# Where two sets of weight sums stand in VectorE's order, in a four-layer attention and gated-unit kernel

## The chip, the core and the metric

The kernel runs on one core of one Trainium2 chip. A core has TensorE (PE) for matrix products, VectorE (DVE), ScalarE (ACT) and GpSimd (POOL) for elementwise work, and queues for DMA, of which SyncE's (SP) issues most transfers here. Each engine works through its own list of instructions in program order, and waits at an instruction until the semaphores it needs have been raised by other engines or by a DMA. The metric is the time of one execution on the device in microseconds (us), as the median of three runs.

## The reference

Four layers are applied to x (2048 rows of 1024): a linear attention and a gated feed-forward, then the same two again with the same weights. Each has a layer norm in front and a residual addition behind.

```python
def attention(x, wqkv, wo):            # 32 heads of 32
    q, k, v = split(x @ wqkv)
    phi = lambda t: where(t > 0, t + 1, exp(t)) + 1e-6
    kv, z = phi(k)^T v, sum over rows of phi(k)
    return (phi(q) kv / (phi(q) z + 1e-6)) @ wo

def gated(x, W_gate, W_up, W_down):    # 1024 -> 3584 -> 1024
    gate = relu(x @ W_gate)
    return (gate * (x @ W_up)) @ W_down

for layer in (attention, gated, attention, gated):
    x = x + layer(layernorm(x), ...)
```

## The kernel before: the parts that matter here

The gated layer computes its products with seven instead of eight block products per 2x2 block (a Winograd scheme), so that TensorE has an eighth less to do. For this each weight block needs sums and differences of its quarters (`make_gu`), and the input needs them too (`sums_x`). The first gated layer works through its first half of rows with sums that it makes itself on VectorE, and stores them to HBM (`tgu`); later passes load them ready-made.

```python
    def make_gu(self, t, w, u):          # sums of weight w ("g" or "u") of unit u
        v = self.nc.vector
        ...
        v.tensor_tensor(out=T[:, 0:2, :, :], in0=..., in1=..., op=ALU.subtract)   # L869, 128x1024
        v.tensor_tensor(out=T[:, 2, :, :], in0=..., in1=T[:, 0, :, :], op=ALU.subtract)  # L871, 128x512
        v.tensor_tensor(out=T[:, 3, :, :], in0=..., in1=T[:, 2, :, :], op=ALU.subtract)  # L872, 128x512
        self.later.at(3, lambda: self.nc.scalar.dma_start(out=self.tgu[w, u], in_=...))
```

`later.at(n, f)` calls f while the program is written, n steps further on (a step is one output tile, or one block product of four matmuls). Within a region the order of an engine's instructions is decided by a scheduler; `behind(it, f, args)` binds what f issues so that it stands after the instruction `it`.

```python
    def behind(self, it, fn, args):
        with self.tc.issue_after(it.ins):
            for a in args:
                fn(a)
```

The output projection of an attention layer makes 24 tiles of 128x512 in three quarters of eight (the last quarter is done differently, later). Each takes eight matmuls into one of four PSUM buffers (`ps`), and VectorE adds it onto the residual. The first quarter goes column half by column half over four row tiles, the others row tile by row tile.

```python
        def out_unit(sc, j, n2):
            t = sc * QT + j
            ps = self.ps.tile([P, NW], F32, tag="a")                 # 4 buffers
            for g in range(G):
                nc.tensor.matmul(ps, lhsT=pqT[sc][...], rhs=T[...], ...)          # L664
            ...
            if t < self.NS:                                          # quarters one and two
                self.last_x = nc.vector.scalar_tensor_tensor(out=xs, in0=ps, ..., in1=x0,
                                                  accum_out=...)                  # L675
            else:                                                    # quarter three
                self.last_x = nc.vector.tensor_tensor(out=xs, in0=x0, in1=ps, op=ALU.add)  # L679
```

Beside these VectorE reduces the attention's denominators (`z_sum`: L621, L622, L623, with GpSimd's products L616 and L628 on either side), finishes means of the layer norm (L205), whose rest is on ScalarE (L208 to L214), and makes the input sums s1 to s4 (`sums_x`: L908 to L911) from the transposed norms.

```python
            for sc in range(1, self.NQ - 1):
                if sc == 1:
                    for j in range(QT):
                        self.ln_at(2 * j + 2, last_ln, QT + j, 2)
                        later.at((11, 13, 15, 16)[j], lambda j=j: self.sums_x(last_ln, 0, j))
                ...
                if sc == 2 and l == 0:
                    for w, n in (("g", 2), ("u", 9)):
                        later.at(n, lambda w=w: self.make_gu(ring.get((last_ln, 0, w, 0)), w, 0))
                run(row_major(out_unit, sc))
```

The gated unit, fourteen block products. The first unit does them in the order one, two, five, six for gate and up in turn; then 7 and 3 for each, then 4 for each.

```python
        def five(w):                       # v = s1 * T0, kept as m5 (V)
            ...
            nc.scalar.activation(out=V[w], in_=v, func=ACT.Copy)
        def one(w):                        # x = first product, copied to y
            ...
            nc.scalar.activation(out=Y[w], in_=X[w], func=ACT.Copy)
        def two(w): ...
        def six(w):
            mm(w, 6, Y[w])
            Z[w] = self.ps.tile([P, NW], F32, tag="a", name=f"z{w}")
            nc.vector.tensor_tensor(out=Z[w], in0=Y[w], in1=V[w], op=ALU.add)     # L971
        ...
        for w in "gu":
            mm(w, 7, Y[w])
            nc.vector.tensor_tensor(out=V[w], in0=Y[w], in1=V[w], op=ALU.add)     # L984
            ...
            mm(w, 3, Z[w])
            ...
        for w in "gu":
            mm(w, 4, Y[w])
            ...
```

The layer around it asks for the weight sums of the next unit, where it has to make them itself:

```python
            for u in range(self.U):
                ...
                ring.load_to(ring.index((l, c, "g", u)) + 5)
                if first:
                    if u + 1 < self.U:
                        self.later.at(4 if u else 8, lambda u=u: behind(
                            self.last_put if u else self.last_x, lambda: [
                            self.make_gu(ring.get((l, c, w, u + 1)), w, u + 1) for w in "gu"]))
```

Of the kernel before, what the change touches and what calls it, by code (L numbers as in the profile page):

```python
# [8 lines left out]
ALU = mybir.AluOpType  # L9
# [80 lines left out]
class _Net:  # L90
# [337 lines left out]
    def layer_A(self, l, last_ln):  # L428
# [363 lines left out]
        with self.tc.manual_schedule(engines={mybir.EngineType.DVE, mybir.EngineType.Pool}):  # L792
            q3 = row_major(q_unit, self.NQ - 1)
            out0 = column_major(out_unit, 0)
            bring = self.bring_back if l else self.load_x
            ring.load_to(ring.index((l, "v1")) + 1)
            m_products(q3.pop(0))
            q3.insert(0, lambda: None)
            later.at(1, lambda: self.behind(ring.last, bring, range(self.NS)))
            for t in range(self.NS, self.ST - QT, 2):  # L800
                later.at(10 + t, lambda t=t: self.behind(self.last_turn, bring, (t, t + 1)))

            def with_fold(u, i):
                return lambda: (u(), fold_wo(i // 2) if i % 2 == 0 else None)

            run(q3[:2])
            run([with_fold(u, i) for i, u in enumerate(q3[2:] + out0[:1])])
            run(out0[1:3])
            ring.free_slowly((l, "o0"), later, 2)
            for i in range(11, self.ST):  # L810
                later.at(1 + 3 * (i - 11), lambda i=i: z_mult(*divmod(i, QT)))
            self.ln_later(last_ln, 0, 2, 2, 2)
            run(out0[3:])
# [5 lines that stand above are left out]
                if sc == 2 and l:  # L819
                    for j in range(QT):  # L820
                        later.at(11 + j, lambda j=j: q_turn(self.NQ - 1, j))
                    for t in range(self.ST - QT, self.ST):
                        later.at(3 + t, lambda t=t: self.behind(self.last_turn, bring, (t,)))
                if sc == 2 and l == 0:
                    for w, n in (("g", 2), ("u", 9)):
                        later.at(n, lambda w=w: self.make_gu(ring.get((last_ln, 0, w, 0)), w, 0))
                run(row_major(out_unit, sc))
            self.pairs = out_pairs(self.NQ - 1)
            self.turns = [] if l else [lambda j=j: q_turn(self.NQ - 1, j) for j in range(QT)] + [
                lambda t=t: self.behind(self.last_turn, bring, (t,)) for t in range(self.ST - QT, self.ST)]  # L830
# [88 lines left out]
    def glu(self, l, c, u, hT):  # L919

        nc, later = self.nc, self.later
        x1, x2 = self.xnT[l, 2 * c], self.xnT[l, 2 * c + 1]
        sa, sb = self.xs[l, c]
        A = {1: x1[:, 0:4, :], 2: x1[:, 4:8, :], 3: sb[:, 4:8, :], 4: x2[:, 4:8, :],
             5: sa[:, 0:4, :], 6: sa[:, 4:8, :], 7: sb[:, 0:4, :]}
        W = {}
        for w in "gu":
            t = self.ring.get((l, c, w, u))
            raw, T = self.raw_gu(t), self.sums_gu(t)
            W[w] = {1: raw[:, 0:4, 0:P], 2: raw[:, 4:8, 0:P], 3: raw[:, 4:8, P:2 * P],  # L930
                    4: T[:, 3, :, :], 5: T[:, 0, :, :], 6: T[:, 2, :, :], 7: T[:, 1, :, :]}

        def mm(w, m, ps, start=False):
            for k in range(4):
                nc.tensor.matmul(ps, lhsT=W[w][m][:, k, :], rhs=A[m][:, k, :],  # L935
                                 start=start and k == 0, stop=k == 3, skip_group_check=True)
            later.tick()

        h = hT[u // 2][:, (u % 2) * 4:(u % 2) * 4 + 4, :]
        V, X, Y, Z, R = {}, {}, {}, {}, {}  # L940

        def relu(out, ps):
            self.last_relu = nc.scalar.activation(out=out, in_=ps, func=ACT.Relu)  # L943

        def put(b, ps):
            self.last_put = nc.vector.tensor_tensor(out=h[:, b, :], in0=ps, in1=R.pop(b), op=ALU.mult)  # L946

        def five(w):
            v = self.kvp.tile([P, NW], F32, tag="kv0" if w == "g" else "kv1", name=f"v{w}")
            mm(w, 5, v, True)  # L950
            V[w] = self.temp(name=f"m5{w}")
            nc.scalar.activation(out=V[w], in_=v, func=ACT.Copy)  # L952

        def one(w):
            X[w] = self.ps.tile([P, NW], F32, tag="a", name=f"x{w}")
            mm(w, 1, X[w], True)
            Y[w] = self.ps3.tile([P, NW], F32, tag="b", name=f"y{w}")
            nc.scalar.activation(out=Y[w], in_=X[w], func=ACT.Copy)

        def two(w):  # L960
            mm(w, 2, X[w])
            if w == "g":
                R[0] = self.temp(name="r0")
                relu(R[0], X[w])
            else:
                put(0, X[w])

        def six(w):
            mm(w, 6, Y[w])
            Z[w] = self.ps.tile([P, NW], F32, tag="a", name=f"z{w}")  # L970
            nc.vector.tensor_tensor(out=Z[w], in0=Y[w], in1=V[w], op=ALU.add)  # L971

        if c == 0 and u == 0:
            for f in (one, two, five, six):
                for w in "gu":
                    f(w)
        else:
            for f, f2 in ((five, one), (two, six)):
                for w in "gu":
                    f(w)  # L980
                    f2(w)
# [3 lines that stand above are left out]
            if w == "g":  # L985
                relu(V[w], V[w])
            else:
                nc.gpsimd.tensor_tensor(out=h[:, 3, :], in0=V["u"], in1=V["g"], op=ALU.mult)  # L988
            mm(w, 3, Z[w])
            if w == "g":  # L990
                R[1] = self.temp(name="r1")
                relu(R[1], Z[w])
            else:
                put(1, Z[w])
        for w in "gu":
            mm(w, 4, Y[w])
            if w == "g":
                R[2] = self.temp(name="r2")
                relu(R[2], Y[w])
            else:  # L1000
                put(2, Y[w])
# [67 lines left out]
    def layer_B(self, l, final):  # L1069
        ring = self.ring  # L1070

        def behind(it, fn):
            with self.tc.issue_after(it.ins):
                fn()

        for c in range(2):
            hT = []
            first = l == 1 and c == 0
            wd = {}
            for u in range(self.U):  # L1080
                if u % 2 == 0:
                    hT.append(self.slot(f"h{l}_{c}_{u // 2}", dtype=F16))
                ring.load_to(ring.index((l, c, "g", u)) + 5)
                if first:
                    if u + 1 < self.U:
                        self.later.at(4 if u else 8, lambda u=u: behind(self.last_put if u else self.last_x, lambda: [
                            self.make_gu(ring.get((l, c, w, u + 1)), w, u + 1) for w in "gu"]))
                    if u in (3, 7):
                        d = self.U - 4 + u // 4 * 2
                        wd[d] = self.load_d(d)  # L1090
                    if 3 < u < 12:
                        self.later.at(4, lambda d=self.U - 4 + (u - 4) // 4 * 2, n=(u - 4) % 4: behind(
                            self.last_put, lambda: self.sums_d(wd[d], d, (n,))))
                if c == 0 and u == 1:
                    for n, turn in enumerate(self.turns):
                        self.later.at(1 + n, turn)
                if c == 0 and u in (1, 2):
                    self.later.at(6, lambda u=u: behind(self.last_put, self.pairs[u - 1]))
                self.glu(l, c, u, hT)
                if c == 0 and u == 2:  # L1100
                    self.pairs[2]()
                if c == 0 and u == (self.U - 1 if first else 0):
                    after = self.last_put.ins
            if c == 0:
                self.ln_chunk(l, 1, 20, 3, 3, after)
            elif not final:
                self.ln_later(l + 1, 0, 28, 6, 4)
            self.down(l, c, hT, final)
# [68 lines left out]
```

## Time and profile before

| | |
|---|---|
| time, median of 3 runs | 1475.59 us (1473.76 to 1477.6) |
| profiled span | 1474.3 us |
| TensorE busy | 1461.8 us, 99% |
| VectorE busy | 842.7 us, 57% |
| ScalarE busy | 578.2 us, 39% |
| GpSimd busy | 285.2 us, 19% |
| weight sums on VectorE (L869) | 28 sets, from 187.2 to 383.0 us |

The profile comes from one execution. Busy time of an engine is a share of the whole span; a matmul of 128x512 takes part in a pipeline, so that its listed duration (379 ns) is longer than the 216 ns after which the next one starts. A row of a table of waits says which engine stood still at which line, and what released it. A row of a table by stretch gives, for each engine, its busy time and its number of instructions in that stretch, then the clock that was granted to TensorE (1.00 is full), the mean busy share of the DMA engines and GB/s.

### The profile page before, as it was taken

To read this page: it belongs to the slowest core of one execution; us is meant where nothing else is said; L and a number is where in the kernel's file an instruction comes from. 1 tells how busy PE (TensorE), PEld (TensorE's weight loads), DVE (VectorE), ACT (ScalarE), POOL (GpSimd) and SP (SyncE) were. 2 spreads that over 40 slices of the span, in tenths; PEclk is the share of its full clock that TensorE was granted. 3 is DMA by queue.
4 is the path that set the end of the run, shared out by engine and by line. 5 is a ranking of instruction groups with operands and counts; after the bars stand their busy time and mean duration, and the time that the engine had idled before them with its cause. 6 is when DMAs were issued, how large, how long until landed. Compare 5 with 4: busy or idle time off the path is not lost.

```text
span 1474.3 us, 18704 instructions
## 1 busy us (share of the span) xinstructions
PE 1461.8 (99%) x6959; PEld 663.5 (45%) x6959; DVE 842.7 (57%) x1483; ACT 578.2 (39%) x1027; POOL 285.2 (19%) x190
## 2 busy tenths in 40 slices
PE   9999989999999999999999999999999999999999
PEld 4444434444444444444444444444444444444444
DVE  7978588666594433346368655766435433443632
ACT  6772564333330233341057726633333203333300
POOL 1354860011100011110023466410111001111000
PEclk9999999999999999999999999999999999999999
DMA  9940769654558954445943019976444687444461
GB/s 257 264 151 11 183 163 223 194 199 158 203 177 239 341 179 130 148 132 185 293 100 72 1 29 266 246 234 197 143 143 150 175 254 256 144 146 147 152 204 43
DMA packets 318363, 255.51 MB, mean 173 GB/s; under 512 B 105792, under 2 KB 291392, under 8 KB 317376
## 3 DMA queue, kind: packets, MB, share of 16 engines
q1 hardware_dynamic: 308304, 234.00, 54.6%
q10 hardware_dynamic: 9968, 20.32, 3.6%
q8 instruction: 54, 0.88, 0.3%
q14 instruction: 37, 0.30, 0.1%
HBM read 195.04 MB, written 34.60 MB: 156 GB/s over the span
## 4 chain that ended last, share of the span: by engine, by line
PE 94%; DVE 3%; DMA 1%; issue 1%; POOL 1%; ACT 0%; SPq 0%; DVEq 0%; POOLq 0%
PE ps L454 13%; PE dy L1034 10%; PE yg L935 10%; PE yu L935 10%; PE dx L1034 7%; PE dv L1034 7%; PE xu L935 6%; PE xg L935 6%; PE ps L664 4%; PE zu L935 3%; PE zg L935 3%; PE vu L935 3%; PE vg L935 3%; PE my L538 3%; PE mv L538 2%; PE mx L538 2%
## 5 line engine op out<-in xcount | busy, mean ns | idle before, releaser
L935 PEld LDWEIGHTS <-w 128*128 128x128 f16 (+1 forms) x3136 | 306.7, 98 | 372.2 <-issue 2.3
L988 POOL TENSOR_TENSOR h<-m5u,m5g 128x512 f16<-128x512 f32 x56 | 71.1, 1270 | 811.7 <-DVE m5u L984 756.4
L454 PE MATMUL ps<-w,xnT 128*128 128x512 bf16 x1024 | 223.6, 379 | 0.7 <-DMA w<-in_A_wqkv_dram 0.5
L1034 PEld LDWEIGHTS <-h 128*128 128x128 f16 x1120 | 109.6, 98 | 132.2
L454 PEld LDWEIGHTS <-xnT 128*128 128x128 bf16 x1024 | 99.4, 98 | 120.8 <-issue 1.5
L971 DVE TENSOR_TENSOR zg<-yg,m5g 128x512 f32<-128x512 f32 x56 | 39.1, 699 | 191.3 <-PE yg L935 191.3
L935 PE MATMUL yg<-s,w 128*128 128x512 f16 x448 | 115.0, 379 | 1.3 <-DVE zg L971 1.2
L935 PE MATMUL xg<-xnT,w 128*128 128x512 f16 x448 | 115.0, 379 | 0.0
L935 PE MATMUL xu<-xnT,w 128*128 128x512 f16 x448 | 115.0, 379 | 0.0
L935 PE MATMUL yu<-s,w 128*128 128x512 f16 x448 | 115.0, 379 | 0.0
L943 ACT ACTIVATE m5g<-m5g 128x512 f32<-128x512 f32 x56 | 35.2, 629 | 189.6 <-DVE m5g L984 189.6
L1034 PE MATMUL dy<-w,h 128*128 128x512 f16 x448 | 98.0, 379 | 0.0
L1034 PE MATMUL dx<-w,h 128*128 128x512 bf16 x448 | 97.3, 379 | 0.0
L401 ACT ACTIVATE e<-e,eps 128x512 f32<-128x512 f32 x128 | 92.4, 722 | 4.2
L400 ACT ACTIVATE e<-ps 128x512 f32<-128x512 f32 x128 | 75.8, 592 | 44.6 <-PE ps L454 43.7
L664 PE MATMUL ps<-T,pqT 128*128 128x512 bf16 x384 | 85.6, 384 | 4.9 <-DVE x L675 4.9
L616 POOL TENSOR_TENSOR kvc<-pq,kvc 128x1024 f32<-128x1024 bf16 x32 | 73.7, 2304 | 66.3 <-DVE den L621 42.3
L952 ACT ACTIVATE m5g<-vg 128x512 f32<-128x512 f32 x56 | 33.4, 597 | 111.7 <-PE vg L935 86.1
L473 POOL TENSOR_TENSOR kvc<-kvc,slab 128x512 f32<-128x512 f32 x46 | 58.0, 1268 | 75.6 <-DVE slab L404 59.6
L946 DVE TENSOR_TENSOR h<-yu,r 128x512 f16<-128x512 f32 x56 | 38.7, 691 | 56.8 <-PE yu L935 56.8
L984 DVE TENSOR_TENSOR m5u<-yu,m5u 128x512 f32<-128x512 f32 x56 | 38.7, 691 | 53.0 <-PE yu L935 53.0
L1034 PEld LDWEIGHTS <-e 128*128 128x128 f16 x448 | 43.9, 98 | 52.8
(154 smaller groups left out, 1966.8 us busy)
## 6 DMA issues: line engine op xcount, KB each, us to landing
w<-in_B_W_gate_dram SPq DMA_DIRECT2D x56, 512.0 KB, 5.8
w<-in_B_W_up_dram SPq DMA_DIRECT2D x56, 512.0 KB, 5.1
w<-td SPq DMA_DIRECT2D x32, 896.0 KB, 4.7
w<-in_B_W_down_dram SPq DMA_DIRECT2D x24, 896.0 KB, 5.2
w<-tg SPq DMA_DIRECT2D x42, 512.0 KB, 6.9
w<-tu SPq DMA_DIRECT2D x42, 512.0 KB, 5.4
w<-in_A_wqkv_dram SPq DMA_DIRECT2D x10, 1024.0 KB, 8.5
away<-x SPq DMA_DIRECT2D x16, 512.0 KB, 4.1
```

Source lines behind the costliest of these rows:

```text
L400: nc.scalar.activation(out=e, in_=ps, func=ACT.Relu, scale=-1.0)
L401: nc.scalar.activation(out=e, in_=e, func=ACT.Exp, scale=-1.0, bias=self.eps6[:, 0:1])
L454: nc.tensor.matmul(by_row(ps), lhsT=self.xnT[l, l_q][:, kt, j * P:(j + 1) * P], rhs=w[:, kt, :].rearrange("p (b i d) -> p i b d", i=R, d=H ...
L473: nc.gpsimd.tensor_tensor(out=ksum[:, cols], in0=ksum[:, cols], in1=pk, op=ALU.add)
L538: nc.tensor.matmul(banks[j], lhsT=A(i)[:, j * P:(j + 1) * P], rhs=B(i), start=start and i == 0, stop=i == NS - 1, skip_group_check=True)
L616: nc.gpsimd.tensor_tensor(out=prod, in0=pq_of[sc, j], in1=zrow, op=ALU.mult)
L664: nc.tensor.matmul(ps, lhsT=pqT[sc][:, g, j * P:(j + 1) * P], rhs=T[g // 4][:, g % 4, n2 * NW:(n2 + 1) * NW], start=(g == 0), stop=(g == G ...
L935: nc.tensor.matmul(ps, lhsT=W[w][m][:, k, :], rhs=A[m][:, k, :], start=start and k == 0, stop=k == 3, skip_group_check=True)
L946: self.last_put = nc.vector.tensor_tensor(out=h[:, b, :], in0=ps, in1=R.pop(b), op=ALU.mult)
L971: nc.vector.tensor_tensor(out=Z[w], in0=Y[w], in1=V[w], op=ALU.add)
L988: nc.gpsimd.tensor_tensor(out=h[:, 3, :], in0=V["u"], in1=V["g"], op=ALU.mult)
L1034: nc.tensor.matmul(banks[j], lhsT=A(k)[:, j * P:(j + 1) * P], rhs=w[:, i, :], start=start and k == 0, stop=k == self.U - 1, skip_group_che ...
```

## The change

Two sets of weight sums get other anchors. The sums of the first gated unit were asked for in the third quarter of the output projection, without an anchor, so that the scheduler was free to place them; now they are asked for in the second quarter, each behind the residual addition that is the latest at that moment. The sums of the second unit were bound to the last residual addition; now they are bound to the latest addition of partial products (L971 in the kernel before) in the first unit, and asked for one step later. For this `six` keeps its addition as `last_z`. The aim is that the sums stand in VectorE's order where their weights have come and nothing urgent is behind them.

```diff
@@ layer_A, around the output projection @@
-                if sc == 2 and l == 0:
-                    for w, n in (("g", 2), ("u", 9)):
-                        later.at(n, lambda w=w: self.make_gu(ring.get((last_ln, 0, w, 0)), w, 0))
+                if sc == 1 and l == 0:
+                    for w, n in (("g", 3), ("u", 10)):
+                        later.at(n, lambda w=w: self.behind(
+                            self.last_x, lambda w: self.make_gu(ring.get((last_ln, 0, w, 0)), w, 0), (w,)))
                 run(row_major(out_unit, sc))
@@ glu, six @@
-            nc.vector.tensor_tensor(out=Z[w], in0=Y[w], in1=V[w], op=ALU.add)
+            self.last_z = nc.vector.tensor_tensor(out=Z[w], in0=Y[w], in1=V[w], op=ALU.add)
@@ layer_B @@
-                        self.later.at(4 if u else 8, lambda u=u: behind(self.last_put if u else self.last_x, lambda: [
+                        self.later.at(4 if u else 9, lambda u=u: behind(self.last_put if u else self.last_z, lambda: [
                             self.make_gu(ring.get((l, c, w, u + 1)), w, u + 1) for w in "gu"]))
```

The lines of the kernel after are one further down from the first edit on (the output projection keeps L664, L675 and L679): L870, L872 and L873 are the weight sums there, L909 to L912 the input sums, L936 the block products, L972 and L985 the additions.

## The prediction

> **What bounds the kernel now.** I read the page first, then the waits of TensorE, then the chain that ended last around the longest wait, then the order of work on VectorE, then tables by stretch.
>
> Parts 1 and 2 of the page: the engine that sets the end, its share of the span, and the clock it was granted in 40 slices.
>
> ```profile
> PE 1461.8 (99%) x6959; PEld 663.5 (45%) x6959; DVE 842.7 (57%) x1483; ACT 578.2 (39%) x1027; POOL 285.2 (19%) x190
> PEclk9999999999999999999999999999999999999999
> ```
>
> TensorE (PE) is busy for 1461.8 of 1474.3 us, so a change off TensorE can save some 12 us at most, plus what TensorE does at less than full speed. The waits of TensorE, with total, number and longest in us:
>
> ```profile
> PE ps L664 <- DVE x L675: 4.9, 2, 2.7
> PE idle L272 <- DVE e L269: 1.3, 1, 1.3
> PE yg L935 <- DVE zg L971: 1.2, 1, 1.2
> ```
>
> Two of them lie where the change acts: 4.9 us in the output projection of the first attention layer (L664, waiting for a residual addition) and 1.2 us in the first gated unit (L935, waiting for zg). The chain that ended last (start, us, what), from 181 us on, says why the first exists:
>
> ```profile
> 181.38 5.83 DMA w<-in_B_W_up_dram
> 187.21 0.02 issue
> 187.23 0.04 DVE w L869
> 187.27 0.57 issue
> 187.84 0.69 DVE x L675 x2
> 188.53 1.13 DVE den L621
> 189.66 0.33 DVE w L871
> 190.00 2.01 DVE den L622
> 192.01 0.33 DVE w L872
> 192.34 0.26 DVE den L623
> 192.60 0.56 DVE x L675 x2
> 193.16 0.04 issue
> 193.21 1.01 PE ps L664 x3
> ```
>
> The first weight sum of the up weights (L869) stands in VectorE's order after three of the eight residual additions of the first quarter. Its operand is still on the way from HBM until 187.2 us. VectorE therefore does nothing from 181.0 to 187.2 us, though the fourth output tile is ready for its addition; the accumulators (four buffers) stay full and TensorE stops for 2.17 us before one tile and 2.73 us before the next. It also costs clock. Busy time by stretch, with the granted clock as last but two figures:
>
> ```profile
> 192.00:194.00 2.00, 0.79 (x3) 0.29 (x3) 1.97 (x9) 0.56 (x1) 1.32 (x1) 0.92 0.39 160
> 194.00:196.00 2.00, 2.00 (x6) 0.76 (x5) 1.93 (x6) 1.87 (x6) 1.38 (x2) 0.50 0.33 119
> 196.00:198.00 2.00, 2.00 (x8) 0.83 (x7) 2.00 (x9) 1.98 (x3) 2.00 (x2) 0.73 0.63 122
> ```
>
> TensorE did six and eight matmuls in stretches in which it does eleven elsewhere.
>
> The best yardstick is in the kernel itself: the second attention layer has the same output projection followed by the same gated unit, but takes its weight sums ready-made from HBM. The same table, from the second output tile to the first gated unit and over that unit, for layer two, layer one, layer one, layer two:
>
> ```profile
> 910.90:950.64 39.74, 39.74 (x197) 18.01 (x185) 31.41 (x76) 26.76 (x54) 21.91 (x11) 1.00 1.03 245
> 175.88:222.52 46.64, 41.73 (x198) 18.41 (x186) 35.87 (x83) 26.19 (x54) 29.80 (x15) 0.96 0.66 150
> 222.52:236.25 13.73, 12.42 (x57) 5.38 (x56) 11.11 (x24) 4.67 (x8) 1.27 (x1) 1.00 1.24 265
> 950.64:962.89 12.25, 12.25 (x58) 5.48 (x57) 7.24 (x14) 4.67 (x8) 1.27 (x1) 1.00 1.11 274
> ```
>
> **What the Trainium skill says.** "DVE: scalar operands, raw-bit mode, write accounting and state across instructions", section Flops that outlive an instruction, calls VectorE's queue one in-order queue; the 6.2 us of idleness in front of ready work agree. "TensorE: Matmul & The Clock Gate", section What's actually happening, says that an idle array falls to half its clock and needs about 3.4 us of work to return; the trace has 0.50 after the two waits, over some 3.2 us (194.0 to 197.0 us, a weight load every 0.43 us instead of 0.21). "SBUF — State Buffer", section Who interferes with whom, says that a VectorE operation with two SBUF inputs and a GpSimd operation exclude each other, and the later one waits for the whole of the other. Here L871, normally 0.42 us, took 2.01 us at 215.36 while GpSimd's L628 ran from 214.92 to 217.08. "VectorE: DVE Perf Modes", section The perf-mode tier table, gives tensor_tensor on 16-bit data in SBUF the double rate, 1224 ns for 2048 elements; the trace has 1.22 us for 2048, 0.68 for 1024 and 0.42 for 512, so one set of three sums is about 1.3 us of VectorE start to start.
>
> **The change part by part.** No instruction is added or removed: 28 sets of sums stay. Only places change, and the order of the changed kernel as built shows them.
>
> (a) Sums of the first gated unit. The up set leaves its place between the third and fourth addition of quarter one. The gate set now follows the first addition of the sixth tile row (tile x6, second quarter), the up set follows both additions of the ninth (x9, third quarter). Both weights were requested at about 181 us and landed at 187; the new places are reached after 193 us and after 205 us, so no wait for HBM remains. What goes is: 2.17 + 2.73 = 4.90 us of waits, the half clock (15 matmuls at 0.43 instead of 0.216 us = 3.2 us, half lost: 1.6), and 0.4 us of restarts and small gaps. The yardstick gives the sum: 46.64 - 39.74 = 6.90 us, if the stretch runs as in layer two. Does it? VectorE there has 31.41 us of work in 39.74 and takes on two sets, 2.6 us; that fits in the total. The gate set falls where VectorE in layer two waits for TensorE by 0.9, 0.15, 0.7 and 1.0 us per addition (930 to 940 us), so with one GpSimd operation of 1.9 us in its way (L628 runs just there, 929.06 to 930.98) it makes additions about 2 us late. Four accumulator buffers of 1.73 us each cover that. The up set falls at the point that corresponds to 941 us, and from there VectorE has no idle time until the input sums are done at 953.7. It pushes these by 1.3 us. The last s1 sum of the inputs starts at 952.20 in layer two, done at 952.62; TensorE wants it for vg at 954.10. Slack 1.5 us, less 1.3 for the up set, less a possible remainder from the gate set and a lock. I charge 0.3 us.
>
> (b) Sums of the second gated unit (two interleaved sets, 237.13 to 239.67 in unit two of the kernel before: 2.54 us). Before, part of them sit between the last input sums and zg, which makes TensorE wait 1.25 us. Now all six follow zu. The unit would run as in layer two (12.25 instead of 13.73 us: 1.48 us), were it not that the six sums now stand in front of the read of yg by m5g (L984). In layer two zu starts at 957.82, so VectorE is free at 958.42; plus 2.54 is 960.96; m5g takes yg until 961.65. TensorE wants to accumulate onto yg again at 961.16. That is 0.5 us of a new wait. The up weights of unit two must be there: their load follows the last normalised transposes, at 945.45 in layer two, 13 us ahead of need, with 5 to 8 us to land. I charge nothing.
>
> (c) Everything after, 1100 us of it, has TensorE at 99% or more and the same orders, so it moves forward by what was gained.
>
> Sum: 6.90 + 1.48 - 0.3 - 0.5 = 7.6 us. 1475.59 - 7.6 = 1468.0 us, 0.5% faster.
>
> **Rivals.**
>
> The lock moves the wait. If a GpSimd operation catches the up set or the gate set leaves VectorE late, the input sums end up to 2 us later and TensorE waits for vg. For it: VectorE is saturated just there, and L908 took 1.87 us at 943.37 beside L628 in layer two. Against it: L628 in front of the up set ends at 941.2, as the set begins. Time then 1469.5 to 1470.
>
> ScalarE becomes the bound. Its eight layer norms run without a break from 193.44 to 217.3 us, and the gated unit needs all eight. If they kept that time, TensorE would wait for them and gain little: about 1473. Against it: their first one waits 14.8 us for a mean that stands behind the stalled VectorE; in layer two they start 8.1 us after the second output tile, which is 184.0 us here, and end 33.2 us after it, at 209.1.
>
> The new place waits for a transfer. VectorE's order has the up sums of unit two directly after zu; if their load, or a store that holds its slot, is late by a few us, m5g and with it TensorE stand still. Time 1470 to 1473. Against: the 13 us above, and the load's issue moves forward along with ScalarE's norms.
>
> Nothing gained. The 4.9 us could have been slack for a later wait; but the other waits in TensorE's table (1.3, 0.6, 0.5 and 0.2 us) lie in the first 31 us, and none is listed after the first gated unit, so I give it little.
>
> **Range and chances.** The most to be had is 8.38 us (both stretches as in layer two), 1467.2; runs of the kernel before scatter over 3.8 us, so the median can lie 1.5 us off: low end 1465.5. The rivals' middle gives the high end, 1472. Two per cent is 29.5 us; neither way is such a change in sight: faster 0.005, within 0.99, slower 0.005.
>
> **What would show it.** Right: no wait of L664 on L675 in TensorE's table; clock 1.00 from 176 us to the gated unit; that unit starting near 215.6 us in place of 222.5; layer norms on ScalarE from about 184; no VectorE wait for the up weights; a wait of about 0.5 us of yg on m5g L985 in place of zg. Wrong: a wait of vg on an input sum of over 1 us, VectorE idle in front of a weight sum until a load lands, or L664 waiting for the additions around the gate set. The prediction fails as a whole if the gated unit starts after 219 us.

## The result, and the profile after

| | before | after |
|---|---|---|
| time, median (lowest to highest) | 1475.75 us (1473.76 to 1477.6) | 1468.79 us (1468.5 to 1468.92) |
| profiled span | 1474.3 us | 1466.7 us |
| TensorE busy | 1461.8 us | 1458.0 us |

The ratio of the times is 0.9953, with a 95% interval of 0.9936 to 0.997: some 7 us less, within 2%. The time was predicted as 1468.0 us (1465.5 to 1472.0).

The first rows of the page of the kernel after, engine totals and granted clock. TensorE (PE) is still busy for 99% of the span. The digits of the clock look as before, for a slice of 37 us is too coarse for a dip of 3 us; its loss shows only in short stretches.

```profile
PE 1458.0 (99%) x6920; PEld 663.1 (45%) x6959; DVE 844.1 (58%) x1483; ACT 578.4 (39%) x1027; POOL 285.8 (19%) x190
PEclk9999999999999999999999999999999999999999
```

TensorE's waits in the kernel after (total, number, longest, in us). The 4.9 us of L664 on L675 are gone, and so are the 1.2 us on zg. In their place stand 0.8 us of L664 on a residual addition of quarter three, and 0.3 us of vg on an input sum; the others of the table lie in the head of the kernel.

```profile
PE ps L664 <- DVE x L679: 0.8, 1, 0.8
...
PE vg L936 <- DVE s L909: 0.3, 1, 0.3
```

The table by stretch of the kernel after: from the second output tile to the first product of the first gated unit, over that unit to the first product of unit two, and two microseconds right behind the gate sums.

```profile
174.90:215.62 40.72, 39.67 (x194) 18.00 (x185) 37.29 (x82) 26.51 (x54) 29.33 (x15) 1.00 0.82 189
215.62:229.34 13.72, 13.47 (x62) 5.76 (x61) 11.44 (x25) 4.78 (x8) 1.27 (x1) 1.00 1.16 231
194.00:196.00 2.00, 2.00 (x11) 0.88 (x10) 1.93 (x3) 2.00 (x4) 0.95 (x1) 1.00 1.00 339
```

The first stretch took 40.72 us in place of 46.64 before and 39.74 in layer two, at full clock, with eleven matmuls in two microseconds where there were six. In layer two TensorE is busy for all of the 39.74 us, so the yardstick is its own work and nothing else. VectorE (DVE) is busy for 37.29 of the 40.72 us, more than in layer two plus two sets of sums (31.41 + 2.6 = 34.0). The prediction gave the unit as the stretch to the last products, one block short of unit two (13.73 and 12.25 us); for a comparison over the whole unit, to the first product of unit two, these are the rows of the kernel before, for layer one and layer two:

```profile
222.52:237.11 14.59, 13.28 (x61) 5.78 (x60) 11.70 (x25) 4.67 (x8) 1.27 (x1) 1.00 1.24 266
950.64:963.75 13.11, 13.11 (x62) 5.87 (x60) 7.84 (x15) 4.67 (x8) 1.27 (x1) 1.00 1.10 282
```

So unit one fell from 14.59 to 13.72 us and did not reach 13.11. From unit two to the end nothing moved: 1474.3 - 237.11 = 1237.2 us before, 1466.7 - 229.34 = 1237.4 after. The two stretches give 5.92 + 0.87 = 6.79 us; the rest of the difference of the profiled spans, 0.98 us, lies ahead of the second output tile (175.88 against 174.90), where the change touches nothing.

What became of VectorE's 34.0 us? One part was there before: layer one's stretch holds seven reductions of denominators (L621, with L622 and L623 behind each), layer two's only six, in both kernels. One such round takes 1.7 us of VectorE. The rest shows in the order of work on VectorE and on GpSimd (POOL), kernel after (start, duration, operation), with the gate set, the up set and the first input sum:

```profile
193.12 2.38 DVE L870 TENSOR_TENSOR w<-w 128x1024 f16<-128x1024 bf16 x1
...
205.28 1.85 DVE L870 TENSOR_TENSOR w<-w 128x1024 f16<-128x1024 bf16 x1
...
210.24 1.88 DVE L909 TENSOR_TENSOR s<-xnT 128x512 f16<-128x512 f16 x1
```

```profile
193.04 1.90 POOL L628 TENSOR_TENSOR pq<-pq,den 128x1024 bf16<-128x1024 bf16 x1
...
204.66 1.92 POOL L628 TENSOR_TENSOR pq<-pq,den 128x1024 bf16<-128x1024 bf16 x1
...
209.92 1.91 POOL L628 TENSOR_TENSOR pq<-pq,den 128x1024 bf16<-128x1024 bf16 x1 [3.34 <-DVE den L623]
```

Each of the three VectorE operations starts inside a product of GpSimd and ends 0.3 to 0.6 us after it. This waiting is called the lock below. Alone they last 0.68, 0.68 and 0.42 us (in the kernel before), so they lost 1.70, 1.17 and 1.46 us. The last of these is no new loss, for in layer two the same sum takes 1.87 us. The gate set was expected to be caught in this way, the up set was not. Together: 31.41 + 2.6 + 1.7 + 1.70 + 1.17 = 38.6 us of work, in a stretch of some 40. VectorE did 37.29 of it in the stretch; the gated unit began with two residual additions fewer done than in layer two (five of L679 against seven).

### The profile page after: what moved, and what is told of

It is laid out like the page before. It is cut to its first block, busy times and chain, and to the rows that moved or that the text cites. A ratio compares the mean times of both kernels' runs of the same rounds, so it can differ in the third digit from the quotient of the medians.

```text
span 1466.7 us, 18659 instructions
## 1 busy us (share of the span) xinstructions
PE 1458.0 (99%) x6920; PEld 663.1 (45%) x6959; DVE 844.1 (58%) x1483; ACT 578.4 (39%) x1027; POOL 285.8 (19%) x190
## 4 chain that ended last, share of the span: by engine, by line
PE 96%; DVE 2%; ACT 0%; issue 0%; DMA 0%; DVEq 0%
PE ps L454 15%; PE dy L1035 10%; PE yg L936 10%; PE yu L936 10%; PE dv L1035 7%; PE dx L1035 7%; PE xg L936 6%; PE xu L936 6%; PE ps L664 4%; PE zu L936 3%; PE zg L936 3%; PE vu L936 3%; PE vg L936 3%; PE my L538 3%; PE mv L538 2%; PE mx L538 2%
## 5 line engine op out<-in xcount | busy, mean ns | idle before, releaser
L936 PEld LDWEIGHTS <-w 128*128 128x128 f16 (+1 forms) x3136 | 306.7, 98 | 371.5 <-issue 1.6
L972 DVE TENSOR_TENSOR zg<-yg,m5g 128x512 f32<-128x512 f32 x56 | 39.2, 699 | 192.7 <-PE yg L936 192.7
L936 PE MATMUL yg<-s,w 128*128 128x512 f16 x448 | 115.0, 379 | 0.1
L936 PE MATMUL yu<-s,w 128*128 128x512 f16 x448 | 115.0, 379 | 0.0
L936 PE MATMUL xg<-xnT,w 128*128 128x512 f16 x448 | 115.0, 379 | 0.0
L936 PE MATMUL xu<-xnT,w 128*128 128x512 f16 x448 | 115.0, 379 | 0.0
L616 POOL TENSOR_TENSOR kvc<-pq,kvc 128x1024 f32<-128x1024 bf16 x32 | 73.6, 2299 | 61.7 <-DVE den L621 37.6
L664 PE MATMUL ps<-T,pqT 128*128 128x512 bf16 x374 | 83.2, 379 | 1.4 <-DVE x L679 0.8
L985 DVE TENSOR_TENSOR m5u<-yu,m5u 128x512 f32<-128x512 f32 x56 | 38.7, 691 | 52.0 <-PE yu L936 52.0
```

The source lines that it names most:

```text
L616: nc.gpsimd.tensor_tensor(out=prod, in0=pq_of[sc, j], in1=zrow, op=ALU.mult)
L664: nc.tensor.matmul(ps, lhsT=pqT[sc][:, g, j * P:(j + 1) * P], rhs=T[g // 4][:, g % 4, n2 * NW:(n2 + 1) * NW], start=(g == 0), stop=(g == G ...
L972: self.last_z = nc.vector.tensor_tensor(out=Z[w], in0=Y[w], in1=V[w], op=ALU.add)
```

## The experiments

Times are medians; "before" in a ratio is the kernel before, run beside. The stretches named are those of the two rows above: second output tile to gated unit, and the unit.

**Is it VectorE's idleness that costs, and how much can it lose for nothing?** The theory: TensorE stops because VectorE stands still ahead of the fourth residual addition, and any occupation of VectorE there does the same, beyond a slack. The rival lays the cost of the old place to the transfers themselves. Three kernels are the kernel after with 5, 10 or 15 statistics of 128x512 (`bn_stats`) put into VectorE's order ahead of the fourth addition. They need nothing from HBM; their output is not used.

```diff
+    if l == 0:                       # N = 5, 10, 15
+        with issue_after(self.last_x.ins):          # third addition
+            for _ in range(N):
+                self.fill = nc.vector.bn_stats(out=fill[:, 0, :], in_=self.x[0][:, 0:NW])
+    # the fourth addition is issued behind self.fill
```

> The kernel after, with five extra BatchNorm statistics (0.60 us each start to start, 3.0 us) put into VectorE's order between the third and fourth residual addition of quarter one, where the up sums stood before. Theory 1, VectorE's order: the fourth addition is then done near 184 us, its buffer is wanted by TensorE near 185.3 us, so no wait: 1468.5 to 1469.5 us. Theory 2, the gain has another source (transfers or stores spread differently, layer norms): also about 1468.8. It sets the zero of the series.

> The same with ten statistics, 6.0 us. Theory 1: the fourth addition ends near 186.7 us, TensorE waits 1.4 us for it and 0.5 us for the next, 1.9 us in two pieces; without a fall of the clock about 1470.7, with one about 1472.3 us. Theory 2: 1468.3 to 1469.5 us, since no transfer is moved.

> The same with fifteen, 9.0 us, about what the kernel before lost there (6.2 us idle, 0.6 us of work, 2.4 us of two more sums and of the lock). Theory 1: TensorE waits 4.3 us and 0.5 us, and the half clock of 1.6 us follows, less up to 1 us of the later waits of the kernel after, which vanish: 1473.8 to 1475.5 us. Theory 2: under 1470.5 us.

| statistics | held on VectorE | time (n) | ratio to before (95%) | stretch |
|---|---|---|---|---|
| none (the kernel after) | 0 | 1468.79 (4) | 0.9953 (0.9936 to 0.997) | 40.72 |
| 5 | 3.61 us | 1471.2 (9) | 0.9974 (0.9964 to 0.9984) | 42.78 |
| 10 | 7.25 us | 1474.43 (12) | 0.9997 (0.9989 to 1.0006) | 46.42 |
| 15 | 10.90 us | 1478.3 (14) | 1.0022 (1.0014 to 1.003) | 50.06 |

A statistic took 0.73 us, start to start, where 0.60 had been expected. TensorE's waits on residual additions in the kernel with five (L676 and L680 are L675 and L679 there) and the place of the one on L676, then the longest in the kernel with ten:

```profile
PE ps L664 <- DVE x L680: 1.8, 2, 1.6
...
PE ps L664 <- DVE x L676: 0.7, 1, 0.7
```

```profile
201.88 10.52 PE L664 MATMUL ps<-T,pqT 128*128 128x512 bf16 x48 [0.72 <-DVE x L676]
```

```profile
PE ps L664 <- DVE x L676: 2.4, 1, 2.4
```

Holding VectorE for 7.25 us, with no transfer in it, brings back the time of the kernel before, where it had stood idle for 6.2. That speaks against the transfers as the cause of the old loss. (Beside the idle time the kernel before had the up sums in that place, and L622 at 2.10 us; the kernel with ten has its sums and their lock later. The two are alike in size, not item by item.) But five were to cost nothing, and that was wrong: they cost 2.06 us of the stretch out of 3.61 (57%), and every five more cost 3.64 us, all that they took. So ten and fifteen also came out above their ranges. VectorE has some 1.5 us to give in this stretch of 40 us, not the depth of four accumulators. With five, VectorE was held from 180.1 to 183.7 us, and TensorE did not wait there at all: on the spot the four accumulators covered 3.6 us. It waited later, 0.72 us at 201 us behind the gate set, and 1.79 us at the additions of quarter three.

The kernels with ten and fifteen also show the clock. The table by stretch, kernel with ten, two stretches of two microseconds after its idle time of 2.45 us, which ended at 188.0 us:

```profile
188.00:190.00 2.00, 2.00 (x7) 0.82 (x7) 1.93 (x4) 0.00 (x0) 0.84 (x1) 0.68 0.00 0
190.00:192.00 2.00, 2.00 (x7) 0.60 (x6) 1.74 (x6) 1.45 (x3) 2.00 (x2) 0.50 0.00 0
```

Seven matmuls in two microseconds, at 0.68 and 0.50 of the clock. This fall added nothing to the time here: the step from five to ten, which brought it, cost 3.64 us, just what the statistics took, and TensorE still waited 1.8 us for VectorE at quarter three.

**One part alone.** The kernel before with only the second unit's sums moved, and the kernel after with only those moved back.

```diff
 # second unit alone: the kernel before, with
-   self.later.at(4 if u else 8, ... self.last_put if u else self.last_x ...
+   self.later.at(4 if u else 9, ... self.last_put if u else self.last_z ...
 # first unit alone: the kernel after, with
-   self.later.at(4 if u else 9, ... self.last_put if u else self.last_z ...
+   self.later.at(4 if u else 8, ... self.last_put if u else self.last_x ...
```

> The kernel before with only the second unit's sums moved behind the additions of partial products. Theory 1: the two waits for the residual additions and the half clock stay (waits of 4 to 5 us in TensorE's table), the wait of 1.2 us for zg goes, 0 to 0.5 us come back as a wait of yg on m5g: 0.7 to 1.2 us under the kernel before, about 1474.7. Rival: this part alone carries the gain, 1469 to 1470 us.

> The kernel after with the second unit's sums put back in front of the additions of partial products. Theory 1: the large gain stays (no wait of several us, clock 1.00), and the wait of yg for zg of about 1.2 us comes back while the small wait behind m5g (0.1 us) goes: 0.6 to 1.3 us over the kernel after, 1469.4 to 1470.1 us. Rival, the two parts do not add up, because what one saves the other would have hidden: 1468.8 within 0.3 us.

| | time (lowest to highest, n) | ratio to before (95%) | first stretch | unit |
|---|---|---|---|---|
| before | | | 46.64 | 14.59 |
| second unit's sums alone | 1474.51 (1473.2 to 1477.36, 12) | 0.9997 (0.9989 to 1.0006) | 46.26 | 13.46 |
| first unit's sums alone | 1470.76 (1469.41 to 1473.57, 6) | 0.9968 (0.9955 to 0.9982) | 40.72 | 14.85 |
| both (after) | 1468.79 (1468.5 to 1468.92, 4) | 0.9953 (0.9936 to 0.997) | 40.72 | 13.72 |

TensorE's waits with the second unit's sums alone moved:

```profile
PE ps L664 <- DVE x L675: 4.5, 2, 2.7
```

and with the first unit's sums alone moved:

```profile
PE yg L936 <- DVE zg L972: 1.2, 1, 1.2
PE ps L664 <- DVE x L679: 0.8, 1, 0.8
```

Each part takes away its own wait and leaves the other one. By the stretches, which leave out what the head of the kernel scatters, the first part is worth 5.92 us and the second 1.13: in the unit the move of the second unit's sums brings 14.59 to 13.46 in one setting and 14.85 to 13.72 in the other, 1.13 both times. The time of the second part alone can't be told from the kernel before, at intervals as wide as one part in a thousand. That of the first part alone, 1470.76 us, lies above its range, 2.0 us over the kernel after, where the stretches account for 1.13; its runs scatter over 4 us, and the one in the profile lost its time in the head (see the end). In the unit of the kernel after 1.13 and the lateness left by the first part (14.85 - 14.59 = 0.26 us) act against each other; 0.87 remains.

**Is the remainder the lock, or are the sums a load of their own?** In the kernel without the last quarter's division, GpSimd does not divide the last quarter of q in layer one by the denominators (L628), the operation that catches the sums. VectorE keeps all its own work. (Lines are one further down there.)

```diff
-                    nc.gpsimd.tensor_tensor(...)                      # L628
+                    if l or sc < self.NQ - 1:
+                        nc.gpsimd.tensor_tensor(...)
```

> The kernel after without GpSimd's four scalings of the last quarter of pq in the first attention layer (L628), so that the last quarter is left undivided by its denominators. Lock theory: L870 of the gate set falls from 2.38 to 0.7 us, that of the up set from 1.85 to 0.7, the first input sum from 1.88 to 0.4; VectorE gets 4.3 us back, and TensorE's waits of 0.84 us on a residual addition and 0.25 us on an input sum go: 1467.5 to 1468.0 us. Rival, VectorE's own added work (2.6 us) makes those waits: durations as before, 1468.6 to 1469.0 us.

Measured: 1466.92 us (1466.73 to 1467.23, 4 runs), 0.9942 (0.9926 to 0.9958). VectorE's order in this kernel, gate set, up set and first input sum as above, then its two stretches:

```profile
193.38 0.68 DVE L871 TENSOR_TENSOR w<-w 128x1024 f16<-128x1024 bf16 x1
...
205.33 0.68 DVE L871 TENSOR_TENSOR w<-w 128x1024 f16<-128x1024 bf16 x1
...
209.13 0.41 DVE L910 TENSOR_TENSOR s<-xnT 128x512 f16<-128x512 f16 x1
```

```profile
175.16:214.89 39.73, 39.52 (x194) 18.00 (x186) 34.98 (x85) 26.42 (x54) 21.83 (x11) 1.00 0.84 196
214.89:228.11 13.22, 13.22 (x62) 5.86 (x61) 9.71 (x21) 4.78 (x8) 1.28 (x1) 1.00 1.16 237
```

Without that GpSimd work the first stretch is 39.73 us, that of layer two to a hundredth (39.74, TensorE's own work), with both sets of sums in it, and no wait of L664 or of vg is listed. So the sums can be free there, and the 0.98 us that the kernel after lacks go with GpSimd's product. (The test is a little generous: it also frees the first input sum, which the lock catches in layer two as well, with 1.87 us.) The unit goes from 13.72 to 13.22, so 0.50 of its remaining 0.61 us goes with it too. What the Trainium skill says in "SBUF — State Buffer", section Who interferes with whom, on which the prediction drew, holds for these sums: at 205 us the same operation takes 1.85 us beside a GpSimd product and 0.68 without one.

**Are earlier places better?** If lateness in front of quarter three costs, the sums might do better further ahead, where more additions follow in which to catch up. One kernel takes the up set from step 10 to 6, the other the gate set from 3 to 1 and the up set from 10 to 5.

```diff
-                    for w, n in (("g", 3), ("u", 10)):
+                    for w, n in (("g", 3), ("u", 6)):      # up earlier
+                    for w, n in (("g", 1), ("u", 5)):      # both earlier
```

> The kernel after with the up set asked for four steps earlier, so that it stands behind the seventh tile row in place of the ninth. If the waits of 0.84 and 0.25 us come from the up set's place in the stretch where VectorE has no idle time, they go: 1467.7 to 1468.2 us. If VectorE's whole work between 193 and 220 us counts, whatever its order, nothing changes: 1468.5 to 1469.1 us.

> The kernel after with both sets earlier, the gate set in front of the fifth tile row's second half and the up set between the two halves of the seventh. As for the run before, in both readings; the locks decide, since the gate set then falls beside another GpSimd operation: 1467.7 to 1469.5 us.

Up set earlier: 1469.26 us (1469.11 to 1469.94, 4 runs), 0.9959 (0.9943 to 0.9975), stretch 41.29. Both earlier: 1471.36 us (1470.9 to 1471.9, 7 runs), 0.9975 (0.9963 to 0.9986), stretch 43.31. The unit took 13.71 in both. Each is slower than its own ranges had it. VectorE's order with both earlier, two of the three gate sums:

```profile
191.24 2.23 DVE L870 TENSOR_TENSOR w<-w 128x1024 f16<-128x1024 bf16 x1
193.50 2.02 DVE L872 TENSOR_TENSOR w<-w 128x512 f16<-128x512 bf16 x1
```

Two GpSimd operations that follow one another caught two sums of one set, so that the set held VectorE for 4.7 us instead of 1.3; the up set was caught twice as well and held it for 4.1. TensorE waited 3.1 us on L675. With the up set alone earlier its first sum took 2.43 us, and TensorE waited 0.6 us on L675 and 0.4 on L679. Earlier was no remedy at these two places; what GpSimd did at the time made the difference.

**A place that the lock leaves alone.** GpSimd goes through L616 and L628 for each denominator, and waits for VectorE's reduction (L621) in between. Sums placed directly ahead of L621 should find GpSimd idle. At step 4 the gate set follows the second addition of tile row six, and the reduction comes next.

```diff
-                    for w, n in (("g", 3), ("u", 10)):
+                    for w, n in (("g", 4), ("u", 10)):     # gate one step later
+                    for w, n in (("g", 4), ("u", 7)):      # and up three steps earlier
```

> The kernel after with the gate set asked for one step later, behind the second addition of the sixth tile row, so that it stands directly in front of a reduction of denominators, when GpSimd has ended its scaling and waits for that reduction. Lock theory: L870 of the gate set takes 0.7 us in place of 2.38, all that follows comes about 1 us earlier, the up set loses some of its 1.2 us too, TensorE's waits of 0.84 and 0.25 us shrink to under 0.5 us together: 1467.6 to 1468.3 us. Rival (the amount of VectorE's work decides): 1468.6 to 1469.1 us.

> The same with the up set also asked for three steps earlier, behind the first addition of the eighth tile row and directly in front of the next reduction of denominators. Lock theory: both sets free of the lock, 3 us of VectorE's time back, and the stretch without idle time relieved of the up set: no wait of TensorE but the lock's 1.5 us on the first input sum left on VectorE: 1467.2 to 1468.0 us. Rival: as the kernel after, or slower as the other earlier placements were (1469.3 to 1471.4 us).

> The kernel after as it is, for comparison on the same chip: 1468.4 to 1469.2 us, with TensorE's waits of 0.8 us on a residual addition and 0.3 us on an input sum.

> The kernel before with a second profile, to see which stretch carries its scatter of some 4 us. Theory 1: the two waits for residual additions depend on the landing of the up weights and differ by a few tenths at most; the scatter then lies in the first 30 us, where TensorE waits for the first loads. Rival: the landing of the up weights differs by some us from execution to execution, and with it the 4.9 us.

| | time (lowest to highest, n) | ratio to before (95%) | first stretch | unit |
|---|---|---|---|---|
| gate 4, up 10 | 1468.08 (1467.72 to 1468.19, 5) | 0.9954 (0.994 to 0.9967) | 40.01 | 13.72 |
| gate 4, up 7 | 1468.4 (1467.91 to 1468.67, 5) | 0.9956 (0.9943 to 0.9968) | 39.97 | 13.71 |
| after, once more | 1468.74 (1468.69 to 1468.87, 5) | 0.9959 (0.9946 to 0.9971) | 40.70 | 13.72 |
| before, once more | 1475.17 (one run) | | 46.12 | 14.61 |

VectorE's order with the gate set at 4 and the up set at 10, first sum of each:

```profile
195.38 0.68 DVE L870 TENSOR_TENSOR w<-w 128x1024 f16<-128x1024 bf16 x1
...
205.40 1.35 DVE L870 TENSOR_TENSOR w<-w 128x1024 f16<-128x1024 bf16 x1
```

GpSimd's last product ahead of the gate set ended at 195.29 us (193.38 + 1.91), 0.09 us before it began, so the set ran at its own speed. VectorE was less late then, and the up set lost 0.7 us instead of 1.2. No wait of L664 is listed. The time is 0.66 us below the kernel after, and the two ranges do not meet: this version is better than both kernels, if by little. The stretch is shorter by as much (40.70 - 40.01 = 0.69 us), so most of what the lock cost there goes with the gate set's place, the up set's smaller loss included.

The kernel with the up set at 7 is a miss in part. The reduction came next there too, but GpSimd had not ended its work: the first sum still took 1.81 us, from 201.26 us, inside a GpSimd product that ran from 200.62. The stretch was as short; the median is 0.3 us higher, with ranges that overlap.

In the second profile of the kernel before, the waits on L675 came to 4.6 us in place of 4.9, a few tenths as the first theory has it. The stretch was 0.52 us shorter and the second output tile came 0.44 us earlier (175.44 against 175.88), so both places carry some of the difference. Two profiles that lie 0.95 us apart can't show where a scatter of 4 us comes from.

## Why the prediction was right

The time is 0.8 us above the predicted one, and the mechanism was as described. The first term of its sum of 7.6 us came out smaller, the net of the second nearly right for other reasons, and one statement under the first was wrong.

**The wait for the up weights and its clock** (the 6.90 us of term a). Right. No VectorE wait for the up weights is left, and the clock is 1.00. That the gated unit starts at 215.62 us, predicted near 215.6, is luck: this execution reached the second output tile 0.98 us earlier than that of the kernel before, and then took 40.72 us for the stretch where 39.74 stood behind the figure. The sum of the lost clock is right in its result, 1.6 us, but not in its count: the weight loads stand 0.43 us apart only from 194.0 to 197.0 us, which is seven or eight matmuls and not fifteen. The statistics show that it was VectorE's standing still that cost the time, and the first unit's sums alone show that this part brings 5.92 us by itself.

**"Four accumulator buffers of 1.73 us each cover that."** This step failed, in size. The gate set lost 1.70 us to the lock as foreseen. But the yardstick holds six rounds of a denominator where layer one has seven, so VectorE's work was 31.41 + 1.7 + 2.6 = 35.7 us and not 34.0. That still "fits in the total", as the kernel without the division shows; with 1.70 and 1.17 us of the lock on top it was 38.6 us of 39.74. VectorE had nearly no room to catch up (five statistics: 1.5 us of slack in 40), so it was late for the next denominator, GpSimd's L628 came later with it, and at 204.66 us it ran into the up set; the prediction had it end just as the up set begins. VectorE ended up behind at quarter three, where L664 waited 0.84 us. In place of a charge of 0.3 us the lock cost 0.98 in the stretch: 5.92 gained of 6.90. The kernel without the division has the whole 6.90, and moving the gate set alone out of the lock brings 0.69 of the 0.98.

**Term b**, the unit: 1.48 us less 0.5 for yg on m5g was expected, 0.87 came. Net it was close, for other reasons. The gap in front of yg was there, for VectorE began m5g only at 226.44 us, behind the six sums, but it did not become a wait: the scheduler had put two vg matmuls of unit two into it, in the order of TensorE in the kernel after:

```profile
226.63 0.59 PE L936 MATMUL vg<-s,w 128*128 128x512 f16 x2
```

The next product starts 0.55 us later, at 227.18; the two take 2 x 0.216 = 0.43 us of it, so about 0.1 us is lost. What took most of the rest was late VectorE: xu to vg started 1.28 us apart (218.28 and 219.56) in place of 0.86, of which 0.25 us is the listed wait on an input sum. The prediction named that wait, but put its charge under term a; without the division it is gone.

**Term c** holds: 1237.2 and 1237.4 us.

**The rivals.** "The lock moves the wait" is what happened in part; its 1469.5 us overrated it, and it named vg, where L664 on L679 took the larger share. ScalarE did not become the bound: its norms moved with the additions, and begin 8.8 us after the second output tile (183.68 us), where layer two gave 8.1.

The new places waited for no transfer: neither L870 of the first unit has idle time in front of it, and in unit two the sums follow zu directly.

Not settled is the last part of a microsecond between the pairs. The profiled runs of both kernels differ by 6.79 us over the stretches in the first pair and by 6.31 in the second (46.12 + 14.61 against 40.70 + 13.72), the medians by 6.96 and 6.22 (1474.96, of nine runs of the kernel before, against 1468.74).

## What to carry to other kernels

When a stage without the trouble exists in the same kernel, it gives the most to be had; but count the operations in both stages before reading slack from it (here one round of a denominator was missing). What a moved operation then gets of it depends on what GpSimd does at that moment. In this kernel the good place for VectorE operations with two SBUF inputs was directly ahead of the VectorE operation that GpSimd was already waiting for; where GpSimd was still at work, the same place did not help. Count an in-order engine's slack in the stretch (here 37.3 of 40.7 us busy, and 1.5 us of slack) and not the buffers behind it: buffers cover a delay once, and only an idle engine makes it good. An operation whose operand comes from HBM should not stand in front of ready work that a saturated engine needs.

## What was not expected of the hardware

- **Clock after short idle times.** In the output projection, one idle time of 2.45 us (ten statistics) was followed by a granted clock of 0.50 to 0.68 from 188 to 192 us, one of 6.09 us (fifteen) by half speed until about 197 us, some 5.5 us. Idle times up to 1.63 us left it at 1.00. One of 2.13 us (both sets earlier) also did: it ended at 205.63 us, and the clock is 1.00 in every two microseconds from 204 to 212 us. So did the first of the two in the kernel before: after its 2.17 us the clock is 1.00 for the 1.9 us up to the next one. Whether there is a limit between 2.17 and 2.45 us, or whether something other than length decides, no run tells.

```profile
205.63 10.52 PE L664 MATMUL ps<-T,pqT 128*128 128x512 bf16 x48 [2.13 <-DVE x L675]
```

- **The lock can be lost twice in a row**: 2.23 and then 2.02 us for sums of 0.68 and 0.42 us. An operation with one tensor as input can be held up too: in the kernel before L622 took 2.10 us, from 189.91 us, beside a GpSimd product that ran from 189.74 to 191.97; in the rest of that stretch it took 0.18 to 0.34 us.
- **Scatter.** The kernel before ranges over 4 us, the kernel after over 0.4. The profiled run of the first unit's sums alone, 1473.57 us, was 4.1 us late already at the second output tile (179.0 against 174.9 us). In its first 14 us TensorE waited 1.8 us for L170, against 0.3, and its matmuls then followed each other at half the pace: six in 2.74 us from 9.13 us, against 1.47 us from 7.39. It began its first long row of matmuls at 13.37 us, against 9.61, which is 3.76 of the 4.1 us. (The column of the granted clock shows 1.00 there all the same, so it does not tell everything.) Why kernels that are the same there scatter differently stays open.
